# The head of an attention and feed-forward kernel on one core: k's maximum from transposes of k itself, parts of k^T v in zeroed tiles, w_out loaded two chunks later, loads issued in the order that the program tells

## The chip, the cores and the metric

The kernel runs on one core of a Trainium2 chip. A core has five engines, each with its own in-order queue of instructions: TensorE (PE; its weight loads are listed apart, as PEld), VectorE (DVE), ScalarE (ACT), GpSimd (POOL) and SyncE (SP), which here only issues DMAs. They meet by semaphores. The metric is the device time of one execution in microseconds (us), the median of several runs. Below, "batch" is the attention's batch (8 of them), and "chunk" is one of the 16 pieces of 128 that the feed-forward's inner width is cut into.

## What is computed

The reference, cut to what matters. Softmax runs over the head dimension for q and over the sequence for k; the result goes through a feed-forward layer with a squared ReLU. Everything is float32, except that w_in and w_out arrive as float64 (read as 64-bit words).

```
batch, n_heads, seq, head_dim = 8, 8, 576, 64        # x: 4608 tokens of 512; d_ff 2048
q_s = exp(q - max(q, axis=-1));  q_s = q_s / (sum(q_s, axis=-1) + 1e-9)
k_s = exp(k - max(k, axis=2));   k_s = k_s / (sum(k_s, axis=2) + 1e-9)
kv  = einsum('bhsd,bhse->bhde', k_s, v)
x   = einsum('bhsd,bhde->bhse', q_s, kv)             # then to (4608, 512)
h   = maximum(x @ w_in, 0.0)
out = h * h @ w_out
```

## The kernel before

**Tiles.** A batch of attention has four pairs of heads (p = 0..3). Of its 576 rows 512 are handled as 128 partitions x 4 rows (`c`), and the last 64 of all heads in "tail" tiles (`kt`, `qt`, `v_tail`). One feed-forward pass t handles 512 tokens: passes 0 to 7 take the main rows of batches 0 to 7, and pass 8 takes the 64-row tails of all batches.

**The feed-forward.** In pass t, for each chunk f, `first` (L467) makes h_f with 12 matmuls (four slices of x times three products of high and low parts: xh·wi_h, xl·wi_h, xh·wi_l). ACT takes the ReLU (r, L478) and the high part of its square (gh, L487); DVE makes the square (L479) and the low part (gl, L488). `second` (L491) adds chunk f-2 into four accumulators with 12 matmuls (gh·wo_h, gh·wo_l, gl·wo_h for each of four rows of tiles). The names in the profile are h, r, gh, gl, acc, with wi and wo for the weights.

**The weights.** Every chunk has one half from w_in ("i") and one from w_out ("o"), 512 KB of float64 each. `load_words` (L105) issues their DMAs on SP. `convert` (L159), called once for each half in turn, emits three steps: `scale_words` (two ACT operations, L125 and L126) for the next half, `join_words` (DVE L133 and L136, then DVE L141 for i or POOL L143 for o) for this one, and `split_words` (ACT cast L152, POOL subtraction L153) for the half before. A matmul of a chunk needs the L152 cast (high part) and the L153 subtraction (low part) of its half. The halves go i0, o0, i1, o1, ....

**The attention.** k's column maximum of a pair: DVE reduces over the four rows of a partition (`k_max`, L287), takes in the tail (L291), and then, for batches 0 and 1, `k_turn_max` (L316) transposes the 128x128 result on PE, reduces it to one column (kc, L322), makes a diagonal (dg, L324, DVE) and `k_shift_pe` multiplies it with ones so that the maximum stands in every partition (kmb, L332); DVE subtracts it (L301, L307). For later batches POOL does the partition maximum (L313). `k_exp` gives ek. `kv_product` (L385) makes k^T v in PSUM, scales it by one over the sum and zeroes the blocks off the diagonal with a mask (L406), and cuts it into kvh (ACT) and kvl (DVE). `x_product` makes x from them.

**What sets the order.** From pass 1 on the instructions stand as the code is written (`manual_schedule`, L636). Before that, for the head (all of batch 0's attention, called the boot, which runs in seven stages over the pairs) and pass 0 with batch 1's attention inside it, a scheduler sets the order of each engine at build time, so code that is moved shows only in the built order. In pass 0, `convert` is called twice for each chunk (L651, L661), and once each for the first four halves after the boot (L573). SP's queue is in order too: a DMA whose buffer is not free holds all that stands behind it. Batch 1's k, q and v have one buffer each, so pair 1's k is loaded when pair 0's ek has been made.

Of the kernel before, what the change touches and what calls it, by code (L numbers as in the profile page):

```python
# [22 lines left out]
def attention_ffn(  # L23
# [26 lines left out]
    P = 128  # L50
# [11 lines left out]
    LW = 2  # L62
    LD = 6
# [24 lines left out]
    mask = const.tile([P, P], F32, tag="mask", name="mask")  # L88
    nc.vector.memset(mask, 0.0)
    for j in range(2):  # L90
        nc.vector.memset(mask[j * D:(j + 1) * D, j * D:(j + 1) * D], 1.0)
# [13 lines left out]
    def load_words(f):  # L105
        pool = const if f < LATE else late
        for name, src in (
            ("i", w_in[:, f * P:(f + 1) * P].rearrange("(kc p) f -> p kc f", p=P)),
            ("o", w_out[f * P:(f + 1) * P, :]),
        ):  # L110
            raw = pool.tile([P, M], U64, tag=f"w{name}{f}", name=f"raw_{name}{f}")
            nc.sync.dma_start(
                out=raw if len(src.shape) == 2 else raw.rearrange("p (a b) -> p a b", b=P),
                in_=src,
            )
            raws.append((name, f, raw))
# [11 lines left out]
    def join_words(m):  # L128
        name, f, raw = raws[m]
        lo, hi = (raw.bitcast(I32).rearrange("p (n t) -> p n t", t=2)[:, :, i] for i in range(2))  # L130
        w = cvt.tile([P, M], I32, tag="w", name=f"w_{name}{f}")
        ps = bank(f"up_{name}{f}").bitcast(I32)
        nc.vector.tensor_scalar(  # L133
            out=ps, in0=hi, scalar1=3, scalar2=None, op0=ALU.logical_shift_left
        )
        nc.vector.scalar_tensor_tensor(  # L136
            out=ps if name == "i" else w, in0=hi, scalar=-(2**31), in1=ps,
            op0=ALU.bitwise_and, op1=ALU.bitwise_or,
        )
        if name == "i":  # L140
            nc.vector.tensor_tensor(out=w, in0=ps, in1=lo, op=ALU.add)  # L141
# [17 lines left out]
    def convert():  # L159
# [29 lines left out]
    def load_kq(b, p, which, queue=nc.sync):  # L189
        t = pair_tile(b, p, [P, 2, C, D], which)  # L190
        src = k if which == "k" else q
        queue.dma_start(
            out=t, in_=src[b, 2 * p:2 * p + 2, 0:M, :].rearrange("h (p c) d -> p h c d", c=C)
        )
# [88 lines left out]
    def k_max(b, p):  # L283
        kr = made["k", b, p]
        tl, th = tail_of(b, p)
        km = small([P, P], "km", f"km_{b}_{p}")
# [10 lines left out]
    def k_shift(b, p, kmx, eng):  # L297
# [17 lines left out]

    def k_turn_max(b, p):  # L316

        km = made.pop(("km", b, p))
        ps = bank(f"kmT_{b}_{p}")
        nc.tensor.transpose(out=ps[:, 0:P], in_=km, identity=ident)  # L320
        kc = small([P, 1], "kc", f"kc_{b}_{p}")
        nc.vector.tensor_reduce(out=kc, in_=ps[:, 0:P], op=ALU.max, axis=AX.X)  # L322
        dg = small([P, P], "dg", f"dg_{b}_{p}")
        nc.vector.tensor_scalar(  # L324
            out=dg, in0=ident, scalar1=kc, scalar2=None, op0=ALU.mult
        )
# [10 lines left out]
    def k_exp(b, p):  # L337
# [47 lines left out]
    def kv_product(b, p):  # L385
# [30 lines left out]
        nc.scalar.copy(out=kvh, in_=kv)  # L416
        nc.vector.tensor_tensor(out=kvl, in0=kv, in1=kvh, op=ALU.subtract)
# [100 lines left out]


# [11 lines left out]
    for f in range(LW):  # L531
        load_words(f)
    x = x_tiles(0)

    def boot_max(p):
        k_max(0, p)
        if p == 0:
            tail_exp(0)

    def boot_turn(p):  # L540
# [5 lines left out]
    def boot_exp(p):  # L546
# [7 lines left out]
        boot_max,  # L554
# [7 lines left out]
    for n in range(len(stages) + NP - 1):  # L562
# [3 lines left out]
        if n == len(stages) - 1:  # L566
# [4 lines left out]
            for f in range(LW, LD):  # L571
                load_words(f)
    for _ in range(2 * LW):  # L573
        convert()
# [59 lines left out]
    for t in range(B + 1):  # L634
        if t == 1:
            ctx.enter_context(tc.manual_schedule())  # L636
# [7 lines left out]
        for f in range(NF):  # L644
# [15 lines left out]
            if t == 0 and f + LW < NF:  # L660
# [47 lines left out]
```

## Time and profile before

| | us |
|---|---|
| median of 3 runs (lowest, highest) | 920.75 (920.45, 921.54) |
| the profiled execution | 920.5 |
| its span, first to last instruction | 918.7 |
| PE busy | 880.0 (96%) |
| DVE busy | 502.4 (55%) |
| ACT busy | 348.9 (38%) |
| POOL busy | 154.7 (17%) |
| mean granted TensorE clock | 0.992 |

The times below are microseconds from the start of the span. Busy shares over the whole span say little here, since the kernel has a head of some 155 us that is unlike the remaining 764 us: the stages have to be read one by one. A row of the timeline gives start, duration, engine, line, operation, what it writes and reads, and how many are merged. Instructions overlap in their pipelines, so the distance from one start to the next is shorter than the duration: two scalings of ACT that follow each other start 0.56 us apart, though each lasts 0.68 us.

### The profile page before, as it was taken

Reading aid. Unit: us, or ns where it says so; the run is one execution under the profiler, and the core shown is the slowest. Engines: PE = TensorE matmul, PEld = TensorE weight load, DVE = VectorE, ACT = ScalarE, POOL = GpSimd, SP = SyncE. Lnnn points to the kernel's source line nnn. Section 1 sums busy time; section 2 is a strip of 40 time slices with the busy share of each in tenths; the row PEclk is TensorE's granted clock in tenths of the full one; section 3 lists DMA queues with packets and bytes.
Section 4 is the critical chain, followed back from the end, with each engine's and each line's share of the span. In section 5 each row is a group of like instructions: output and inputs, shape, how many; then the busy total and the mean of one; then the engine's idle time right before and its main releaser. Section 6 shows DMA issues by size and latency. Waiting matters only on the chain.

```text
span 918.7 us, 11463 instructions
## 1 busy us (share of the span) xinstructions
PE 880.0 (96%) x4136; PEld 731.2 (80%) x4136; DVE 502.4 (55%) x982; ACT 348.9 (38%) x679; POOL 154.7 (17%) x238
## 2 busy tenths in 40 slices
PE   3598999999999999999999999999999999999997
PEld 2486778888888888888888888888888888888886
DVE  8978888654564447545745466454744442233222
ACT  3997445333343234333433343333423332232221
POOL 3366663101111111111111101111110100000000
PEclk9799999999999999999999999999999999999999
DMA  8990102111221122111311031112211020001001
GB/s 247 355 381 25 38 24 84 35 35 34 59 81 35 35 53 86 35 34 32 95 36 35 15 101 35 35 35 58 81 35 35 1 97 1 1 8 39 0 1 47
DMA packets 84937, 57.38 MB, mean 62 GB/s; under 512 B 53520, under 2 KB 78096, under 8 KB 84752
## 3 DMA queue, kind: packets, MB, share of 16 engines
q1 hardware_dynamic: 83168, 55.33, 19.6%
q10 hardware_dynamic: 1712, 1.31, 0.5%
q8 instruction: 33, 0.54, 0.2%
q14 instruction: 24, 0.20, 0.1%
HBM read 46.14 MB, written 10.49 MB: 62 GB/s over the span
## 4 chain that ended last, share of the span: by engine, by line
PE 81%; DVE 8%; ACT 7%; issue 2%; DMA 1%; POOL 1%; SPq 0%; DVEq 0%; ACTq 0%
PE h L473 38%; PE acc L495 37%; PE kv L391 2%; PE x L428 2%; PE qT L368 1%; DVE xl L464 1%; DVE gl L488 1%; ACT r L478 1%; DVE h L479 1%; ACT gh L487 1%; ACT raw_i L125 1%; ACT raw_i L126 1%; ACT raw_o L125 1%; DVE km L287 1%; ACT raw_o L126 1%
## 5 line engine op out<-in xcount | busy, mean ns | idle before, releaser
L473 PE MATMUL h<-xh,wi 128*128 128x512 f32 x1152 | 382.8, 395 | 5.3 <-ACT wi L152 5.0
L495 PE MATMUL acc<-wo,gh 128*128 128x512 f32 x1152 | 349.6, 390 | 3.5 <-ACT gh L487 3.4
L473 PEld LDWEIGHTS h<-xh,wi 128*128 128x128 f32 x1152 | 217.1, 189 | 53.1 <-ACT wi L152 5.9
L495 PEld LDWEIGHTS acc<-wo,gh 128*128 128x128 f32 x1152 | 215.1, 188 | 49.7 <-ACT gh L487 5.7
L473 PE MATMUL h<-xl,wi 128*128 128x512 f32 x576 | 225.7, 392 | 0.0
L495 PE MATMUL acc<-wo,gl 128*128 128x512 f32 x576 | 217.4, 389 | 0.0
L479 DVE SCALAR_TENSOR_TENSOR h<-h,r 128x512 f32<-128x512 f32 x144 | 100.6, 698 | 193.4 <-ACT r L478 192.7
L488 DVE TENSOR_TENSOR gl<-h,gh 128x512 fp32r<-128x512 f32 x144 | 99.5, 691 | 171.5 <-ACT gh L487 168.1
L478 ACT ACTIVATE r<-h 128x512 f32<-128x512 f32 x144 | 86.0, 597 | 219.2 <-PE h L473 219.1
L487 ACT ACTIVATE gh<-r 128x512 fp32r<-128x512 f32 x144 | 91.0, 632 | 196.8 <-PE acc L495 194.1
L495 PEld LDWEIGHTS acc<-wo,gl 128*128 128x128 f32 x576 | 108.0, 188 | 22.6
L473 PEld LDWEIGHTS h<-xl,wi 128*128 128x128 f32 x576 | 108.9, 189 | 20.8
L301 POOL TENSOR_TENSOR k<-k,kmx 128x512 f32<-128x512 f32 x24 | 31.0, 1291 | 172.6 <-issue 172.6
L313 POOL PARTITION_ALL_REDUCE kmx<-km x24 | 17.6, 734 | 226.8 <-DVE km L291 221.1
L391 PEld LDWEIGHTS kv<-v,ek 128*128 128x128 f32 x256 | 33.4, 195 | 4.5 <-ACT wi L152 2.4
L391 PE MATMUL kv<-v,ek 128*128 128x129 f32 x256 | 34.8, 279 | 2.2 <-ACT wi L152 2.0
L287 DVE TENSOR_REDUCE km<-k 128x128 f32<-128x512 f32 x32 | 33.9, 1059 | 2.7 <-DMA k<-in_k_dram 2.7
L342 ACT ACTIVATE ek<-k 128x512 f32<-128x512 f32 x32 | 20.1, 627 | 23.6 <-POOL k L301 16.7
L382 DVE TENSOR_TENSOR ql<-qT,qh 128x512 fp32r<-128x512 f32 x32 | 22.0, 688 | 6.8 <-ACT qh L381 6.8
L416 ACT CAST kvh<-kv 128x128 fp32r<-128x128 f32 x32 | 9.5, 298 | 39.3 <-DVE kv L406 39.1
L240 DVE TENSOR_REDUCE mx<-q 128x8 f32<-128x512 f32 x32 | 21.7, 679 | 2.7 <-DMA q<-in_q_dram 2.3
L464 DVE TENSOR_TENSOR xl<-x,xh 128x512 fp32r<-128x512 f32 x32 | 20.2, 687 | 5.4 <-ACT xh L463 5.3
(84 smaller groups left out, 675.2 us busy)
## 6 DMA issues: line engine op xcount, KB each, us to landing
k<-in_k_dram SPq DMA_DIRECT2D x32, 256.0 KB, 2.8
v<-in_v_dram SPq DMA_DIRECT2D x64, 128.0 KB, 3.1
raw_i<-in_moe_w_in_dram SPq DMA_DIRECT2D x16, 512.0 KB, 8.1
raw_o<-in_moe_w_out_dram SPq DMA_DIRECT2D x16, 512.0 KB, 7.9
out_dram<-o SPq DMA_DIRECT2D x32, 256.0 KB, 2.6
q<-in_q_dram SPq DMA_DIRECT2D x28, 256.0 KB, 2.9
q<-in_q_dram ACTq DMA_DIRECT2D x4, 256.0 KB, 4.7
kt<-in_k_dram SPq DMA_DIRECT2D x16, 64.0 KB, 2.7
```

What stands on the lines that cost most here:

```text
L240: nc.vector.tensor_reduce(out=mx, in_=t, op=ALU.max, axis=AX.X)
L287: nc.vector.tensor_reduce(out=km.rearrange("p (h d) -> p h d", h=2), in_=kr.rearrange("p h c d -> p h d c"), op=ALU.max, axis=AX.X,)
L301: eng.tensor_tensor(out=kr, in0=kr, in1=kmx.rearrange("p (h d) -> p h d", h=2).unsqueeze(2).broadcast_to([P, 2, C, D]), op=ALU.subtract,)
L382: nc.vector.tensor_tensor(out=ql[:, 0:M], in0=ps, in1=qh[:, 0:M], op=ALU.subtract)
L391: nc.tensor.matmul(out=ps[:, 0:W], lhsT=kr[:, c, :], rhs=vr[:, c, :], start=(c == 0), stop=False)
L464: nc.vector.tensor_tensor(out=lo, in0=src[:, p, :], in1=hi, op=ALU.subtract)
L473: nc.tensor.matmul(out=ps, lhsT=w[f][:, p * P:(p + 1) * P], rhs=m, start=(n == 0), stop=(n == 3 * NP - 1))
L478: nc.scalar.activation(out=r, in_=ps, func=AF.Relu)
L479: nc.vector.scalar_tensor_tensor(out=ps, in0=ps, scalar=0.0, in1=r, op0=ALU.max, op1=ALU.mult)
L487: nc.scalar.activation(out=gh, in_=r, func=AF.Square)
L488: nc.vector.tensor_tensor(out=gl, in0=ps, in1=gh, op=ALU.subtract)
L495: nc.tensor.matmul(out=acc[c], lhsT=a[:, cs], rhs=w[f], start=(f == 0 and n == 0), stop=(f == NF - 1 and n == 2),)
```

## The change

Four things are changed, all in the head and in what it shares with later batches.

1. **k's maximum.** For batches 0 and 1, `k_max` goes. k is loaded as (row, head, d) instead of (head, row, d), so that each of the four rows of a pair is a 128x128 block; PE transposes all four into one PSUM bank (kT), and one DVE reduction over 512 gives the column kc. The tail's maximum comes from two transposes for each batch (`k_tail_max`, ktT and ktm), and is taken in by an operation on 128x1. The diagonal dg is made by ACT. The subtraction and division of q's tail move from DVE to POOL for these batches.
2. **k^T v.** The mask goes. Two pairs of tiles, kvh and kvl, are zeroed once by POOL; ACT writes the scaled 64x64 diagonal blocks into kvh, and DVE the rest into kvl, straight from PSUM. This holds for all eight batches.
3. **Halves.** The list `halves` goes i0, i1, i2, o0, i3, o1, ...: w_out's half of a chunk stands behind w_in's half two chunks later. Four halves are loaded early, eight more in the boot, then two in each chunk; the first four conversions are called in the last stages of the boot, and i0 and i1 are joined with POOL.
4. **DMA issues.** SP follows the written order from the start of the program.

The core of the diff (before.py to after.py):

```diff
+    EARLY = 4
+    AHEAD = 12
...
+    halves = [("i", f) for f in range(LA)]
+    for f in range(NF):
+        halves += [("i", f + LA)] * (f + LA < NF) + [("o", f)]
+    def load_words(n):
+        for name, f in halves[len(raws):len(raws) + n]:
...
+        on_vector = name == "i" and f >= LA
-        if name == "i":
+        if on_vector:
             nc.vector.tensor_tensor(out=w, in0=ps, in1=lo, op=ALU.add)
         else:
             nc.gpsimd.tensor_tensor(out=w, in0=w, in1=lo, op=ALU.add)
...
+        turned = which == "k" and b < 2
+        t = pair_tile(b, p, [P, C, 2, D] if turned else [P, 2, C, D], which)
...
+        rows_max(qt, G, f"t{b}", nc.vector if b > 1 else nc.gpsimd)
...
+    def k_tail_max(b):
+        ps = bank(f"ktT_{b}")
+        for i in range(2):
+            nc.tensor.transpose(
+                out=ps[:, i * P:(i + 1) * P],
+                in_=made["kt", b][:, 2 * i:2 * i + 2, :].rearrange("p h d -> p (h d)"),
+                identity=ident,
+            )
+        ktm = small([P, NP], "ktm", f"ktm_{b}")
+        nc.vector.tensor_reduce(
+            out=ktm, in_=ps[:, 0:2 * P].rearrange("p (n t) -> p n t", t=TL), op=ALU.max, axis=AX.X
+        )
     def k_turn_max(b, p):
-        km = made.pop(("km", b, p))
-        nc.tensor.transpose(out=ps[:, 0:P], in_=km, identity=ident)
+        kr = made["k", b, p].rearrange("p c h d -> p c (h d)")
+        for c in range(C):
+            nc.tensor.transpose(
+                out=ps[:, c * P:(c + 1) * P], in_=kr[:, c, :], identity=ident
+            )
-        nc.vector.tensor_reduce(out=kc, in_=ps[:, 0:P], op=ALU.max, axis=AX.X)
+        nc.vector.tensor_reduce(out=kc, in_=ps, op=ALU.max, axis=AX.X)
+        nc.vector.tensor_tensor(
+            out=kc, in0=kc, in1=made["ktm", b][:, at:at + 1], op=ALU.max
+        )
-        nc.vector.tensor_scalar(
-            out=dg, in0=ident, scalar1=kc, scalar2=None, op0=ALU.mult
-        )
+        nc.scalar.activation(out=dg, in_=ident, func=AF.Copy, scale=kc)
...
+        kvh, kvl = kv_parts[(b * NP + p) % 2]
         for j in range(2):
+            at = slice(j * D, (j + 1) * D)
+            one = ps[at, j * (D + 1):j * (D + 1) + D]
+            nc.scalar.activation(out=kvh[at, at], in_=one, func=AF.Copy, scale=ks[at])
             nc.vector.scalar_tensor_tensor(
...
+                out=kvl[at, at], in0=one, scalar=ks[at], in1=kvh[at, at],
+                op0=ALU.mult, op1=ALU.subtract,
             )
...
+    order = ExitStack()
+    order.enter_context(tc.manual_schedule(engines={mybir.EngineType.SP}))
...
             load_v(1, 0)
-            for f in range(LW, LD):
-                load_words(f)
-    for _ in range(2 * LW):
-        convert()
+            load_words(AHEAD - EARLY)
+        if n >= len(stages) + NP - 1 - EARLY:
+            convert()
...
-            if t == 0 and f + LD < NF:
-                load_words(f + LD)
-            if t == 0 and f + LW <= NF:
+            if t == 0:
+                load_words(2)
                 convert()
```

Where the scheduler puts things, at the two places that matter most below. The first is ACT's queue just ahead of the cast of chunk 0's w_in half (wi0); a name like raw_i3 is the float64 words of w_in's half for chunk 3, xh_0_3 the high part of x of pair 3 of batch 0, kvh1 the second zeroed tile. Before:

```order
L126 ACTIVATE raw_i3_382<-raw_i3_382 128x512
L447 COPY xt_0_329<-x_0_2_1_440 128x64
L125 ACTIVATE raw_o3_384<-raw_o3_384 128x512
L126 ACTIVATE raw_o3_384<-raw_o3_384 128x512
L435 CAST xh_0_3_158<-x_0_3_0_458 128x288
L435 CAST xh_0_3_158<-x_0_3_1_464 128x224
L125 ACTIVATE raw_i4_386<-raw_i4_386 128x512
L126 ACTIVATE raw_i4_386<-raw_i4_386 128x512
L125 ACTIVATE raw_o4_388<-raw_o4_388 128x512
L126 ACTIVATE raw_o4_388<-raw_o4_388 128x512
L125 ACTIVATE raw_i5_390<-raw_i5_390 128x512
L152 CAST wi0_488<-w_i0_476 128x512
```

and in the changed program:

```order
L457 CAST xh_0_0_160<-x_0_0_0_328 128x288
L457 CAST xh_0_0_160<-x_0_0_1_334 128x224
L408 CAST qh_0_2_429<-qT_0_2_424 128x512
L133 ACTIVATE raw_i1_154<-raw_i1_154 128x512
L408 CAST qh_0_1_347<-qT_0_1_342 128x512
L134 ACTIVATE raw_i1_154<-raw_i1_154 128x512
L435 ACTIVATE kvh0_93<-kv_0_2_353,ks_0_2_359 64x64
L133 ACTIVATE raw_i2_156<-raw_i2_156 128x512
L134 ACTIVATE raw_i2_156<-raw_i2_156 128x512
L469 COPY xt_0_340<-x_0_0_1_334 128x64
L161 CAST wi0_455<-w_i0_406 128x512
```

The cast of wi0 stood behind the scaling of ten halves and a half (i0 to o4, and the first step of i5), and now stands behind three (i0, i1, i2); it also stands ahead of all casts of x but pair 0's.

The second place is SP's queue from the twelfth weight half on; x_tail is the store of the tails of x, v_tail the load of batch 1's tail of v, k_1_1 and v_1_1 the loads of pair 1 of batch 1. Before, all weight loads but one stood ahead of x_tail and of pair 1:

```order
L112 DMA raw_o5_392<-in_moe_w_out_dram 128x512
L223 DMA v_tail_98<-in_v_dram 64x2x64 x4
L112 DMA raw_i6_554<-in_moe_w_in_dram 128x4x128
L112 DMA raw_o6_556<-in_moe_w_out_dram 128x512
L112 DMA raw_i7_616<-in_moe_w_in_dram 128x4x128
```

Now:

```order
L123 DMA raw_o4_400<-in_moe_w_out_dram 128x512
L471 DMA x_tail_103<-xt_0_340 512x1x64
L232 DMA v_tail_104<-in_v_dram 64x2x64 x4
L121 DMA raw_i7_561<-in_moe_w_in_dram 128x4x128
L123 DMA raw_o5_563<-in_moe_w_out_dram 128x512
L121 DMA raw_i8_627<-in_moe_w_in_dram 128x4x128
L123 DMA raw_o6_629<-in_moe_w_out_dram 128x512
L203 DMA k_1_1_648<-in_k_dram 128x8x64
L203 DMA q_1_1_650<-in_q_dram 128x2x256
L121 DMA raw_i9_678<-in_moe_w_in_dram 128x4x128
L123 DMA raw_o7_680<-in_moe_w_out_dram 128x512
L210 DMA v_1_1_739<-in_v_dram 128x4x64 x2
```

Twenty weight halves now stand behind x_tail, which waits for the whole boot; sixteen of them stand behind k_1_1, which waits for ACT to make pair 0's ek of batch 1, and fourteen behind v_1_1, which waits for PE's k^T v of that pair.

The third place is ACT's queue around the ReLU of chunk 5 (r_0_5), in the changed program; x_1 is the copy of x for the next pass, wo3 and wi6 the casts of weights.

```order
L133 ACTIVATE raw_i10_769<-raw_i10_769 128x512
L134 ACTIVATE raw_i10_769<-raw_i10_769 128x512
L500 ACTIVATE r_0_5_917<-h_0_5_904 128x512
L133 ACTIVATE raw_o8_771<-raw_o8_771 128x512
L134 ACTIVATE raw_o8_771<-raw_o8_771 128x512
L464 COPY x_1_536<-x_1_0_0_799 128x288
L161 CAST wo3_780<-w_o3_745 128x512
```

At chunk 5 before, ACT had all 32 halves scaled; now the scaling of i10 and o8 stands ahead of the cast of wo3, which PE needs as soon as h_5 is done.

More of the change, by code (lines that the diff above doesn't have):

```diff
@@ L87, in attention_ffn @@
     nc.vector.memset(ones, 1.0)
[L88 to L91, printed above, removed]
+    zeros = const.tile([P, P], F32, tag="zeros", name="zeros")
+    nc.gpsimd.memset(zeros, 0.0)
+    kv_parts = []
+    for i in range(2):
+        kv_parts.append([const.tile([P, P], F32R, tag=f"kv{c}{i}", name=f"kv{c}{i}") for c in "hl"])
+        for part in kv_parts[-1]:
+            nc.gpsimd.tensor_copy(out=part, in_=zeros)
     dram = ctx.enter_context(tc.tile_pool(name="dram", bufs=1, space=bass.MemoryType.DRAM))
@@ L103, in attention_ffn @@
     raws = []
[L105 to L114, printed above, removed]
-            )
+    halves = [("i", f) for f in range(LA)]
[3 more added lines that the diff above has]
+        for name, f in halves[len(raws):len(raws) + n]:
+            raw = (const if f < LATE else late).tile(
+                [P, M], U64, tag=f"w{name}{f}", name=f"raw_{name}{f}"
+            )
+            if name == "i":
+                src = w_in[:, f * P:(f + 1) * P].rearrange("(kc p) f -> p kc f", p=P)
+                nc.sync.dma_start(out=raw.rearrange("p (a b) -> p a b", b=P), in_=src)
+            else:
+                nc.sync.dma_start(out=raw, in_=w_out[f * P:(f + 1) * P, :])
             raws.append((name, f, raw))
@@ L189, in load_kq @@
     def load_kq(b, p, which, queue=nc.sync):
[L190 to L193, printed above, removed]
-        )
+        turned = which == "k" and b < 2
+        t = pair_tile(b, p, [P, C, 2, D] if turned else [P, 2, C, D], which)
+        src = (k if which == "k" else q)[b, 2 * p:2 * p + 2, 0:M, :]
+        to = "p c h d" if turned else "p h c d"
+        queue.dma_start(out=t, in_=src.rearrange(f"h (p c) d -> {to}", c=C))
         made[which, b, p] = t
@@ L285, in k_max @@
         tl, th = tail_of(b, p)
-        km = small([P, P], "km", f"km_{b}_{p}")
+        km = small([P, P], "km", f"km_{b}_{p}", 1)
         nc.vector.tensor_reduce(
@@ L530, in attention_ffn, with boot_turn @@
         load_v(0, p)
-    for f in range(LW):
-        load_words(f)
+    load_words(EARLY)
     x = x_tiles(0)
-    def boot_max(p):
-        k_max(0, p)
+    def boot_turn(p):
         if p == 0:
+            k_tail_max(0)
             tail_exp(0)
-    def boot_turn(p):
         k_turn_max(0, p)
@@ L635, in attention_ffn @@
         if t == 1:
+            order.close()
             ctx.enter_context(tc.manual_schedule())
@@ L659, in attention_ffn @@
                 step_after(b, f, x_next)
-            if t == 0 and f + LW < NF:
+            if t == 0:
                 convert()
```

52 lines of the change are left out of this document (19 added, 33 removed).

## The prediction

> **What bounds the kernel now.** I read first the busy times by stage, then PE's timeline at the borders of the stages, then who PE waits for between them. The first view: columns are length, then busy time and count of PE, PEld, DVE, ACT and POOL, the granted clock, the DMA share and GB/s.
>
> ```profile
> 0.00:41.90 41.90, 16.92 (x95) 13.65 (x95) 37.51 (x107) 26.68 (x60) 13.56 (x30) 0.90 0.93 291
> 41.90:50.60 8.70, 8.70 (x28) 6.40 (x28) 8.21 (x15) 8.30 (x16) 8.70 (x8) 0.68 1.06 399
> 50.60:68.50 17.90, 17.85 (x87) 14.73 (x86) 12.98 (x24) 17.90 (x36) 9.36 (x11) 1.00 1.07 385
> 68.50:155.00 86.50, 79.88 (x376) 64.37 (x375) 74.17 (x141) 46.11 (x90) 52.12 (x50) 1.00 0.12 33
> 155.00:918.70 763.70, 756.68 (x3556) 632.01 (x3554) 369.55 (x699) 249.87 (x481) 71.00 (x142) 1.00 0.14 42
> ```
>
> From 155 on PE is busy 756.7 of 763.7 us at full clock, and nothing in the change takes a matmul out of that stage: it stays as it is. All that can move lies ahead of 155. There PE is idle 25 us before 41.9, and 6.6 us between 68.5 and 155.
>
> PE's timeline at the borders: the first feed-forward matmul, the end of the first two chunks (h_0, h_1), and the point where pass 0 has been added up and pass 1 runs on alone.
>
> ```profile
> 41.89 0.80 PE L473 MATMUL h<-xh,wi 128*128 128x512 f32 x1 [4.30 <-ACT wi L152]
> 50.34 0.38 PE L332 MATMUL kmb<-dg,ones 128*128 128x128 f32 x2
> 155.02 0.39 PE L473 MATMUL h<-xh,wi 128*128 128x512 f32 x1
> ```
>
> The first matmul waits for ACT's cast of wi0, and ACT's timeline shows why that is late:
>
> ```profile
> 20.13 0.68 ACT L125 ACTIVATE raw_i<-raw_i 128x512 f32<-128x512 f32 x1
> 20.69 0.68 ACT L126 ACTIVATE raw_i<-raw_i 128x512 int32<-128x512 uint32 x1
> ...
> 40.52 0.24 ACT L447 COPY xt<-x 128x64 f32<-128x64 f32 x1
> 40.62 0.72 ACT L125 ACTIVATE raw_i<-raw_i 128x512 f32<-128x512 f32 x1
> 41.18 0.65 ACT L152 CAST wi<-w_i 128x512 fp32r<-128x512 f32 x1
> ```
>
> The words of i0 were scaled at 20.13, and cast 21 us later; ACT scaled other halves meanwhile. DVE, 37.5 of 41.9 us busy, was late as well: it made w_i0 only at 40.19 (next fence). So the head is bound by the order of work on ACT and DVE, not by loads.
>
> **The change, term 1: the first two chunks come earlier.** The built order has wi0's cast behind 3 scaled halves instead of 10.5. Two scaling steps start 0.56 us apart (20.13 and 20.69), so a half is 1.12 us and 7.5 halves are 8.4 us of ACT. The casts of x of pairs 1 to 3 and their neighbours, some 3.3 us, also stand behind it now. On ACT alone the cast could stand at 41.2 - 8.4 - 3.3 = 29.5. DVE must keep up:
>
> ```profile
> 40.19 0.67 DVE L141 CUSTOM_DVE_ANT_0 w_i<-raw_i,up_i 128x1024 uint16<-128x1024 uint16 x1
> L287 DVE TENSOR_REDUCE km<-k 128x128 f32<-128x512 f32 x32 | 33.9, 1059 | 2.7 <-DMA k<-in_k_dram 2.7
> L291 DVE TENSOR_TENSOR km<-km,kt 64x128 f32<-64x128 f32 x32 | 9.1, 285 | 1.5 <-DMA kt<-in_k_dram 0.6
> L324 DVE TENSOR_SCALAR dg<-ident,kc 128x128 f32<-128x128 f32 x8 | 4.9, 608 | 0.2
> L322 DVE TENSOR_REDUCE kc<-kmT 128x1 f32<-128x128 f32 x8 | 2.3, 283 | 1.0 <-PE kmT L320 0.9
> L240 DVE TENSOR_REDUCE mx<-q 128x8 f32<-128x512 f32 x32 | 21.7, 679 | 2.7 <-DMA q<-in_q_dram 2.3
> L241 DVE TENSOR_TENSOR qt<-qt,mx_t 128x256 f32<-128x256 f32 x8 | 3.4, 422 | 0.2
> L153 POOL TENSOR_TENSOR wi<-w_i,wi 128x512 fp32r<-128x512 f32 x16 | 20.7, 1295 | 2.7 <-ACT wi L152 2.7
> ```
>
> Ahead of w_i0 DVE loses five L287 (1.06 each), five L291 (0.28), four L324 (0.61) and four operations on q's tail (0.42, as L241): 10.8 us. It gains four kc over 512 elements instead of 128; no row shows that reduction from PSUM, so I take L240's 0.68 for the same 128x512 (bounds: 0.28, as now, and L287's 1.06), and a few short ones: 4 x 0.4 + 0.9 = 2.5 us. Some 7 us of batch 1's reductions and other halves' joins move behind w_i0. That is 15 us less: w_i0 at about 26, POOL's addition after it (1.3 us, as its 128x512 subtraction) at 27.5. ACT's 29.5 is the later of the two. The dg on ACT (four) and the split kvh (two 64x64 for one 128x128) are not in the trace; between the 0.24 of L447 and the 0.65 of a 128x512 cast I take 0.25 each, 2 us, most of it in ACT's idle time before 20. **First matmul at 30** (28 to 33).
>
> PE then runs h_0 and h_1 over pairs 0 to 2 and waits for pair 3, whose casts stand behind i3 and o1 on ACT: three more halves (3.4 us), the wi1 cast and the 3.3 us from above put xh_3 at 36 to 37, DVE's low part 0.7 behind, and the last matmuls at **39** (37 to 43), against 50.34 + 0.2 = 50.6. **Term 1: -11.6.**
>
> **Loads.** A k load now lands in pieces of 256 bytes instead of 1 KB. The first window below holds mostly 1 KB pieces, the second v alone, in 256-byte pieces; the last three columns are clock, DMA share, GB/s.
>
> ```profile
> 8.00:11.00 3.00, 0.41 (x2) 0.18 (x1) 3.00 (x7) 1.76 (x4) 0.55 (x1) 1.00 1.07 319
> 11.50:15.00 3.50, 0.39 (x1) 0.18 (x1) 3.44 (x8) 1.26 (x2) 1.04 (x1) 1.00 0.59 133
> ```
>
> For the same busy engines v moves 133/0.59 = 225 GB/s against 319/1.07 = 298. Four k loads of 0.26 MB then take 4.7 instead of 3.5 us: 1.2 us, hidden behind DVE, which by the new order takes q's two maxima (0.68 and about 0.4) ahead of the first kc; without that cover it costs the 1.2 us. The Trainium skill, "DMA: Bandwidth & Descriptors", section Specifications, says that line rate needs pieces of at least 512 B; the trace agrees in direction (225 against 298), and by it alone the change would start about 1 us later, which is inside the range of term 1.
>
> **Term 2: more on PE.** Batch 0's extra transposes fall into PE's idle time. Batch 1's, inside pass 0, are on the path: 12 more for the four pairs and 2 for the tail.
>
> ```profile
> 95.40 0.44 PE qT L368 x4
> ```
>
> Four transposes took 0.44 in the chain of waits; twelve are 1.3 us (the tail's two run while PE waits for pair 3). **Term 2: +1.3.**
>
> **Term 3: the waits of pass 0.** Between 50.5 and 155 PE waits for these, longest first:
>
> ```profile
> PE acc L495 <- ACT gh L487: 3.4, 3, 1.8
> PE kv L391 <- ACT wi L152: 2.0, 1, 2.0
> PE h L473 <- ACT wi L152: 0.7, 1, 0.7
> PE kmb L332 <- DVE dg L324: 0.3, 1, 0.3
> PE kv L391 <- issue: 0.2, 1, 0.2
> ```
>
> That is 6.6 us. I walked the new order by hand with the durations above and four more from the chain of waits (start, length, engine, tile, line):
>
> ```profile
> 63.05 0.53 ACT gh L487
> 65.80 0.47 ACT r L478
> 67.84 0.52 ACT wo L152
> 101.36 0.85 PE x L428 x6
> ```
>
> Five waits stand out. (a) After h_1 ACT still has r_0, r_1, the scaling of i5, gh_0 and wo0's cast, 2 x 0.47 + 1.12 + 0.53 + 0.52 = 3.1 us, and PE only 0.5 us of transposes: 2.5 us. (b) wo1's low part is POOL's third task in a row of 1.3 us: 1 to 2. (c) Around chunk 5 ACT has i10 and o8 ahead of wo3's cast: PE has x_product's 0.85 us and waits 2 to 3. (d) The same at chunk 9 with wo7: 1.5 to 2.5. (e) At the end of pass 0 the last x_product now stands right before the matmuls of pass 1 that read it, and its copy, cast and low part take 1.7; before, 2.7 us of matmuls lay in between. Sum 8.7 to 11.7; I take 9.5, and the old 6.6 go. **Term 3: +2.9** (-4 if PE finds ACT ahead everywhere but in (a), +6 at the upper ends with late loads).
>
> The late loads: the told order holds 20 halves behind x_tail, and 16 of them behind pair 1's k.
>
> ```profile
> 56.70 1.97 SPq L449 DMA_DIRECT2D x_tail<-xt  x1
> DMA to landing us min/median/max: 4.3/8.1/9.5
> ```
>
> x_tail's issue took 1.97 us and a w_in half landed 4.3 us after its issue at best. With x_tail released at about 39, i7 lands at 48, when ACT reaches it at 46 to 47. Pair 1's k is released by ek at 56, and i9 lands at 62; ACT, behind chunk 4's ReLU, would reach it at 59. ACT so waits 1.5 and 3 us, with everything in its queue behind; (c) includes that. The second hold (pair 2's, i13) is alike, and (d) includes it.
>
> **Term 4: later passes.** The split kvh and kvl hand over four times instead of twice, a chunk before x_product reads them: nothing (bounds -0.3 and +1.5). DVE and ACT have half their time free there.
>
> **Sum.** -11.6 + 1.3 + 2.9 = -7.4 against this execution's own 920.5 (span 918.7 and 1.8 around it; the median of the runs is 920.75): **913**.
>
> **Rivals.** (1) *PE finds its operands ready.* DVE is 10 us lighter, so the joins may run far ahead; then only (a) and (e) remain: waits of 4.2, -12.7: 908. For it: DVE was the one 74 of 86.5 us busy in that stage. Against it: ACT's new row keeps scaling to chunk 10. (2) *The change does little:* DVE or a late k keeps w_i0 until 36. Then term 1 is -6 and the sum -2: 918.5. For it: DVE was nearly never idle before 40. (3) *Slower:* the told order starves ACT. If each of the four held groups (behind x_tail, and pairs 1, 2 and 3's k and v) costs PE 5 us instead of 1 to 3, waits are 20 or more; it turns slower when they pass 9.5 + 7.4 = 17. Released a chunk late (6.8 us) twice: 913 + 13.6 = 926.5. For it: SP's queue is in order and ACT's too, so one late half stops ReLUs behind it; against it: between 68.5 and 155 the DMA share is 0.12, so a released load goes at once. (4) *PE at half rate.* The clock by the granted-clock column:
>
> ```profile
> 30.00:32.00 2.00, 0.80 (x4) 0.59 (x4) 2.00 (x7) 1.65 (x7) 1.08 (x1) 1.00 1.07 379
> 34.00:36.00 2.00, 1.33 (x4) 0.98 (x4) 2.00 (x5) 2.00 (x6) 0.00 (x0) 0.50 1.05 407
> 46.00:48.00 2.00, 2.00 (x7) 1.59 (x6) 1.97 (x5) 1.88 (x4) 2.00 (x3) 0.64 1.04 391
> 48.00:50.00 2.00, 2.00 (x11) 1.65 (x10) 1.68 (x3) 1.72 (x4) 2.00 (x2) 1.00 1.05 404
> ```
>
> After a thin stretch from 29 the clock fell to 0.50, and came back 5 us after matmuls ran densely; 13 matmuls then cost 0.2 us more each. The new head has thin stretches too, and (a) is one: half rate over the first three chunks would add 13 x 0.2 and as much again, less what the waits hide, about 3.5 us: 916.5. The Trainium skill, "TensorE: Matmul & The Clock Gate", section "What's actually happening", puts the fall at an idle window of about 3.4 us; (a)'s 2.5 would be just short of it, and the trace's fall after five thin microseconds fits.
>
> **How the numbers follow.** Forecast 913: 0.60; (1) 908: 0.14; (2) 918.5: 0.10; (3) 926.5: 0.07; (4) 916.5: 0.09. The forecast's own range, from the bounds of terms 1 and 3, is 908 to 918. The range 906.5 to 919.5 takes in (1), (2) and (4) with their spread, and leaves out (3) and the edges. A measurement can tell 0.2%, 1.8 us: faster than 918.7 are the forecast, (1), (4) and half of (2), 0.88, less 0.03 for the forecast's upper tail: 0.85; within 0.2% that tail and the other half of (2), 0.08; slower (3), 0.07.
>
> **What would show it.** First h matmul at 28 to 33 and the end of h_1 at 37 to 43; (a) of 2 to 3 us on PE before the first acc, for wo0's cast; waits for wo3 and wo7 after chunks 5 and 9; SP idle before k_1_1 for ek; pass 1's lone stretch from about 147.5 instead of 155.02; the rest of the span 763.7 as now. It would be wrong if h_0 starts after 35, if pass 0's waits exceed 14 us, or if the stage after it changes length by over 2 us.

## The result: slower, 928.03 us, and the profile after

The changed kernel takes **928.03 us** (median of 5, 927.62 to 928.50) against 921.54 for the kernel before (median of 5, 920.45 to 924.20): ratio **1.0067, 95% interval 1.0050 to 1.0085**. The profiled execution has a span of 925.8, against 918.7. The forecast was 913, with a range up to 919.5.

The busy times by stage of the changed kernel, with the columns as in the prediction:

```profile
0.00:32.10 32.10, 19.12 (x102) 16.39 (x102) 24.46 (x69) 19.59 (x44) 16.96 (x38) 1.00 0.92 236
32.10:41.50 9.40, 9.06 (x36) 7.11 (x36) 8.86 (x23) 9.32 (x23) 5.95 (x6) 0.82 0.96 354
41.50:68.50 27.00, 23.23 (x103) 18.45 (x102) 18.28 (x35) 21.42 (x43) 13.00 (x14) 0.94 0.64 198
68.50:155.00 86.50, 79.75 (x369) 65.13 (x369) 74.28 (x129) 54.56 (x107) 53.13 (x50) 0.96 0.33 104
155.00:925.80 770.80, 762.53 (x3555) 633.45 (x3555) 367.03 (x675) 260.10 (x506) 71.82 (x143) 1.00 0.15 42
```

The clock column is below 1.00 in the three stages from 32.10 to 155, where the kernel before had it below 1.00 only ahead of 50.6, and the last stage is 7.1 us longer. PE's timeline at the borders and at its waits (the wait and who ended it stand in brackets):

```profile
32.15 0.50 PE L495 MATMUL h<-xh,wi 128*128 128x512 f32 x1 [2.43 <-DVE xl L458]
40.93 0.60 PE L344 MATMUL kT<-ident,k 128*128 128x128 f32 x4
43.93 1.90 PE L517 MATMUL acc<-wo,gh 128*128 128x512 f32 x4 [2.40 <-ACT wo L161]
70.25 0.37 PE L450 MATMUL x<-qh,kvh 128*128 128x288 f32 x1 [3.02 <-DVE kvl L436]
72.21 0.58 PE L450 MATMUL x<-qh,kvh 128*128 128x288 f32 x1 [1.32 <-ACT x L464]
101.34 0.37 PE L450 MATMUL x<-qh,kvh 128*128 128x288 f32 x1 [1.19 <-DVE w_o L145]
103.27 0.38 PE L450 MATMUL x<-qh,kvh 128*128 128x288 f32 x1 [1.29 <-DVE w_i L150]
156.04 0.50 PE L495 MATMUL h<-xh,wi 128*128 128x512 f32 x1 [1.90 <-ACT xh L485]
```

The head came as forecast: h_1 ends at 40.9 and not at 50.3, 9.4 us earlier. To see where that went I take a mark that both kernels have, the two transposes of q's tail in chunk 2 of pass 1 (the first fence is the kernel before, the second the changed one; the second line of each is the group of all such transposes, whose last is in pass 6):

```profile
163.87 0.38 PE L268 MATMUL qTt<-ident,qt 128*128 128x128 f32 x2
L268 PE MATMUL qTt<-ident,qt x16: 270/271/476, 17.8 to 653.1; 128*128 128x128 f32 x16
```

```profile
167.15 0.39 PE L277 MATMUL qTt<-ident,qt 128*128 128x128 f32 x2
L277 PE MATMUL qTt<-ident,qt x16: 270/273/474, 11.6 to 658.7; 128*128 128x128 f32 x16
```

So the changed kernel is 9.4 ahead at the end of h_1, 3.3 behind at the start of pass 1, 5.6 behind in pass 6 and 7.1 behind at the end. **Pass 0 gives back 12.7 us, and the passes behind it, which I had at nothing, lose another 3.8.**

**Pass 0.** PE's groups between 41 and 165, with the idle time ahead of each (the last figures of a row):

```profile
L495 PE MATMUL h<-xh,wi 128*128 128x512 f32 x137 | 47.7, 412 | 2.0 <-ACT xh L485 1.9
L517 PE MATMUL acc<-wo,gh 128*128 128x512 f32 x130 | 45.5, 419 | 2.7 <-ACT wo L161 2.7
L495 PE MATMUL h<-xl,wi 128*128 128x512 f32 x68 | 27.9, 410 | 0.2 <-DVE xl L486 0.2
L450 PE MATMUL x<-qh,kvh 128*128 128x288 f32 x8 | 2.9, 359 | 6.8 <-DVE kvl L436 3.0 <-ACT x L464 1.3 <-DVE w_i L150 1.3
```

That is 11.7 us, 5.1 more than the 6.6 before, and the largest part stands ahead of x_product, which waited for nothing in the kernel before. Then the clock, in the three stretches behind the longest waits:

```profile
44.00:48.00 4.00, 3.90 (x10) 2.60 (x11) 4.00 (x7) 4.00 (x9) 2.80 (x3) 0.57 0.65 174
70.00:80.00 10.00, 8.42 (x28) 6.83 (x29) 7.10 (x13) 8.59 (x18) 5.37 (x6) 0.66 0.39 150
156.00:162.00 6.00, 5.74 (x17) 4.39 (x18) 3.83 (x8) 1.86 (x4) 1.04 (x1) 0.72 0.55 197
```

(1 - 0.57) x 4 + (1 - 0.66) x 10 + (1 - 0.72) x 6 = 6.8 us, of which some 0.3 is idle time counted already. In the kernel before the same column was 1.00 from 50.6 on. With the 1.3 us of more transposes (the forecast's figure) and 0.5 for slower matmuls (next) that makes 5.1 + 6.5 + 1.3 + 0.5 = 13.4, near the 12.7 that the marks show. The clock's share in it is worked out and not tested: no run changes the clock alone.

**The later passes.** The chain of waits in pass 7, in which there is no attention, of the changed kernel and then of the kernel before (start, length, matmuls). The first row is h of chunk 12; the accumulation of a chunk comes two chunks later, so that the last row is the accumulation of chunks 13 to 15:

```profile
805.52 2.80 PE h L495 x12
808.32 2.75 PE acc L517 x12
...
822.18 2.80 PE h L495 x12
824.98 8.40 PE acc L517 x36
```

```profile
799.56 2.72 PE h L473 x12
802.28 2.72 PE acc L495 x12
...
815.88 2.72 PE h L473 x12
818.60 8.16 PE acc L495 x36
```

From the start of the first row to the end of the last it is 27.86 us against 27.20. The matmuls that use the weights of chunks 12 to 15 are issued 3% more slowly (233 ns for 227), in every pass, with no wait between them and the clock at 1.00; the chunks ahead run as before, but for the accumulation rows between such rows (2.75), whose ends border on them. From the mark in pass 1 to that in pass 6 it is 0.46 us a pass; 8 passes of 0.46 to 0.66 make 3.7 to 5.3, which covers the 3.8 that the later passes lost.

### The profile page after: what moved, and what is told of

Read it like the earlier page. It is cut to its first block, busy times and chain, and to the rows that moved or that the text cites. A ratio compares the mean times of both kernels' runs of the same rounds, so it can differ in the third digit from the quotient of the medians.

```text
span 925.8 us, 11627 instructions
## 1 busy us (share of the span) xinstructions
PE 893.7 (97%) x4164; PEld 740.5 (80%) x4164; DVE 492.9 (53%) x927; ACT 365.0 (39%) x719; POOL 160.9 (17%) x249
## 4 chain that ended last, share of the span: by engine, by line
PE 87%; ACT 6%; DMA 3%; DVE 2%; issue 1%; SPq 0%; POOL 0%; DVEq 0%; ACTq 0%
PE acc L517 40%; PE h L495 40%; PE x L450 2%; PE kv L418 2%; PE qT L395 1%; DMA k<-in_k_dram 1%; ACT raw_i L133 1%; ACT raw_i L134 1%; DMA raw_o<-in_moe_w_out_dram 1%; DMA raw_i<-in_moe_w_in_dram 1%; ACT raw_o L133 1%; ACT raw_o L134 1%; ACT r L500 1%; ACT gh L509 1%; PE kv L421 0%
## 5 line engine op out<-in xcount | busy, mean ns | idle before, releaser
L517 PE MATMUL acc<-wo,gh 128*128 128x512 f32 x1152 | 361.4, 393 | 2.7 <-ACT wo L161 2.7
L517 PE MATMUL acc<-wo,gl 128*128 128x512 f32 x576 | 225.8, 392 | 0.0
L435 ACT ACTIVATE kvh<-kv,ks 64x64 fp32r<-64x64 f32 x64 | 19.8, 310 | 39.5 <-PE qT L395 20.1
L436 DVE SCALAR_TENSOR_TENSOR kvl<-kv,ks,kvh 64x64 fp32r<-64x64 f32 x64 | 18.1, 283 | 20.9 <-ACT kvh L435 20.5
L450 PE MATMUL x<-qh,kvh 128*128 128x288 f32 x64 | 19.7, 311 | 7.4 <-DVE kvl L436 3.0
L296 DVE TENSOR_REDUCE km<-k 128x128 f32<-128x512 f32 x24 | 25.6, 1065 | 0.5 <-DMA k<-in_k_dram 0.5
```

The source lines that it names most:

```text
L296: nc.vector.tensor_reduce(out=km.rearrange("p (h d) -> p h d", h=2), in_=kr.rearrange("p h c d -> p h d c"), op=ALU.max, axis=AX.X,)
L450: nc.tensor.matmul(out=ps[:, 0:SH], lhsT=a, rhs=c[:, cs], start=(j == 0), stop=(j == 2))
L517: nc.tensor.matmul(out=acc[c], lhsT=a[:, cs], rhs=w[f], start=(f == 0 and n == 0), stop=(f == NF - 1 and n == 2),)
```

## The experiments

The ratios are each to the kernel before in the same comparison.

| kernel | us | ratio (95%) |
|---|---|---|
| changed | 928.03 | 1.0067 (1.0050 to 1.0085) |
| pad | 927.25 | 1.0077 (1.0064 to 1.0089) |
| before_off | 925.22 | 1.0053 (1.0041 to 1.0066) |
| pad256 | 922.99 | 1.0022 (1.0011 to 1.0033) |
| kold | 929.54 | 1.0082 (1.0065 to 1.0099) |
| kvold | 919.99 | 0.9987 (0.9975 to 0.9998) |
| halold | 917.63 | 0.9963 (0.9951 to 0.9976) |
| free_sp | 933.58 | 1.0145 (1.0132 to 1.0159) |
| ahead16 | 928.63 | 1.0093 (1.0080 to 1.0107) |
| a16d | 921.65 | 0.9995 (0.9982 to 1.0008) |
| kv16 | 916.43 | 0.9949 (0.9936 to 0.9963) |
| **kv16d** | **915.41** | **0.9937 (0.9925 to 0.9950)** |
| hal16d | 916.39 | 0.9951 (0.9935 to 0.9966) |

### Where the late weights lie: pad, before_off, pad256

Chunks 12 to 15 are those whose weights lie in the pool `late`, allocated behind the small pool `tiny`. The change puts a new small tile, ktm, into `tiny`: two slots of 32 bytes. That moves `late`, and with it the tiles of the boot, which lie in the same place until `late` is opened. The addresses of wi12 in the built programs, in bytes of a partition:

```
before      190720 = 745 x 256          pad         189312 = 739 x 256 + 128
changed     189248 = 739 x 256 + 64     before_off  190784 = 745 x 256 + 64
                                        pad256      189440 = 740 x 256
```

The edit is one number, here that of pad (48 in before_off too, 80 in pad256); the instructions and their order stay the same:

```
-    tiny.tile([P, 32], F32, tag="pad2", name="pad2")
+    tiny.tile([P, 48], F32, tag="pad2", name="pad2")
```

> The changed kernel with the small pool made 64 bytes longer, so that the late pool (the parts of wi12 to wo15) starts on a multiple of 128 bytes again, as it did before; the order of all instructions is the same. Theory A (addresses): the 24 matmuls of each of chunks 12 to 15 are issued 231 ns apart in the changed kernel and 227 in the kernel before; 96 x 9 passes x 4.5 ns = 3.9 us, so 924.1 (928.03 - 3.9), and the last 20 us back to 227 ns. Rival (the later passes are longer through the split kv parts' extra handovers and the wait for ks): no change, 928, chunks 12 to 15 stay at 231.

> The kernel before with the small pool made 64 bytes longer, so that its late pool starts 64 bytes beside a multiple of 128; the order of all instructions is the same. Theory A: chunks 12 to 15 go from 227 to 231 ns a matmul, +3.9 us, 925.4 against 921.5. Rival (the addresses are without effect; the edits of k and kv cost it): 921.5.

pad did not do what theory A said: 927.25, and its last accumulation in pass 7 still takes 8.40. before_off did: 4.9 us slower by the ratio. That row of before_off, from its chain of waits:

```profile
823.66 8.40 PE acc L495 x36
```

So the address matters, but a multiple of 128 isn't enough. The constants' weights lay on multiples of 256 in both kernels, hence:

> As pad, but the small pool is 192 bytes longer than in the changed kernel, so that wi12 to wo15 start on a multiple of 256 bytes, as all weights of the kernel before did (with 128 bytes beside such a multiple, in pad, their matmuls stayed at 231 ns). Same order of instructions as the changed kernel. Theory A, mended (the weights want a multiple of 256 bytes): chunks 12 to 15 at 227 ns in all passes, 3.9 us less, 924.1, and from pass 1's first qTt to the end as long as before, 655 instead of 658.6. Rival (something else than the address, e.g. the split kv parts): 928.

pad256 came as forecast, with the same row back at the old length:

```profile
820.40 8.16 PE acc L517 x36
```

From the mark in pass 1 to the end of the span it takes 755.4 us; the changed kernel took 758.65 (925.8 - 167.15), the kernel before 754.8 (918.7 - 163.87). The rest of the gain, some 1 to 2 us, lies ahead of the mark (165.11 against 167.15), where the same waits came out a little otherwise; before_off lost 2.6 us there, with a half-clock stretch at 118 to 122 that the kernel before did not have. Why is open.

### The parts one by one: kold, kvold, halold

kold and kvold undo one part each in pad256; halold undoes one more in kvold.

```
kold     -  transposes of the four blocks of k, ktT, dg on ACT, k loaded as "p c h d"
         +  k_max on DVE, one transpose a pair, dg on DVE, k loaded as "p h c d"
kvold    -  kvh[at, at] on ACT and kvl[at, at] on DVE for each of two blocks, tiles zeroed once
         +  kv with the mask on DVE, kvh one cast on ACT, kvl one difference on DVE
halold   -  i0, i1, i2, o0, i3, o1, ...
         +  i0, o0, i1, o1, ...
```

> pad256 with k's maximum as before the change (on DVE over k as loaded in long pieces, one transpose a pair, diag on DVE); the told order, the parts of kv and the order of the halves stay. If the new maximum brings the early head (my term 1), the first h comes at 36 to 38 instead of 32 and the time is 4 to 6 us above pad256; rival (the order of the halves alone brings it, and the 12 transposes and ACT's diag cost): the first h stays near 32 and the time is 1 to 3 us below pad256.

kold: the first feed-forward matmul moves from 31.73 in pad256 to 42.58, later than forecast, and the time rises by 0.60%, 5.5 us. The new maximum makes the early head. It is worth half of what the head gains: of the 10.9 us only 2.5 are left at the mark in pass 1 (165.11 in pad256, 167.60 in kold), and 4.9 more come behind the mark in these two executions, which differ by 7.4, where kold waits for batch 2's ek (see ahead16 below). k_max is a boot stage of its own again in kold, as before the change.

```profile
42.58 0.63 PE L488 MATMUL h<-xh,wi 128*128 128x512 f32 x1
```

> pad256 with the parts of k^T v as before the change (masked product on DVE, one cast on ACT, one difference on DVE); the rest stays. If the handovers ACT-DVE-ACT-DVE of the split parts hold x_product in pass 0 (PE waits 3.0 for kvl at 67 to 70 in the changed kernel), that wait falls to below 1 and the time is 2 to 4 us below pad256. Rival (that wait is ACT's wait for i9, told order): within 1.5 us of pad256, the wait stays.

kvold: 0.35%, 3.2 us faster than pad256, and faster than the kernel before. The group of x_product in pass 0 waits 0.6 us in place of 6.8 in the changed kernel, though ACT's wait for raw_i is no shorter (4.0 us, 3.8 in pad256), so the rival is out:

```profile
L452 PE MATMUL x<-qh,kvh 128*128 128x288 f32 x8 | 2.6, 320 | 0.6 <-ACT kvh L440 0.6
```

The timelines of ACT and DVE in the changed kernel show how the split parts wait (two fences, ACT and then DVE):

```profile
66.55 0.30 ACT L435 ACTIVATE kvh<-kv,ks 64x64 fp32r<-64x64 f32 x1
66.76 0.65 ACT L133 ACTIVATE raw_o<-raw_o 128x512 f32<-128x512 f32 x1
...
68.49 0.31 ACT L435 ACTIVATE kvh<-kv,ks 64x64 fp32r<-64x64 f32 x1
```

```profile
67.41 0.27 DVE L436 SCALAR_TENSOR_TENSOR kvl<-kv,ks,kvh 64x64 fp32r<-64x64 f32 x1
...
69.81 0.29 DVE L436 SCALAR_TENSOR_TENSOR kvl<-kv,ks,kvh 64x64 fp32r<-64x64 f32 x1
```

Four operations of 0.3 us take from 66.55 to 70.10, since other work (scaling of weights and gh on ACT, joins and gl on DVE) stands between the two on each engine, and PE's x_product at 70.25 needs the last. In the profiled executions kvold reaches the mark 3.9 us before pad256 (161.19) and gives 2.6 of them back behind it.

> kvold with the halves in the order before the change (i0, o0, i1, o1, ...) in place of the new one, in which halves of w_out stand two chunks later. If the new order brings the early head, wi1 is now a half later and h_1 ends 2 us or more after kvold's 41.1, and the time is 2 to 4 us above kvold, 922 to 924. Rival (the new order only moves the wait from wi1 to wo0, at the first acc): h_1 ends later, the wait before the first acc falls from 3.4 to about 1, and the time is within 1.5 us of kvold.

halold: 0.24%, 2.2 us faster than kvold, with intervals that just overlap. Neither time came: the first theory had it slower, the rival within 1.5 us. The first acc of kvold, and then that of halold:

```profile
45.09 3.41 PE L519 MATMUL acc<-wo,gh 128*128 128x512 f32 x8 [3.37 <-ACT gh L511]
```

```profile
45.63 2.42 PE L519 MATMUL acc<-wo,gh 128*128 128x512 f32 x8
```

The last matmul of h_1 starts at 40.89 in kvold and at 45.21 in halold, and yet the accumulation starts at 45.09 and 45.63: what the new order gains at h_1, PE waits for the square of h. In these executions halold reaches the mark 0.5 us later than kvold (161.73), and its gain lies behind it (755.7 us to the end against 758.0). So the 2.2 us are not shown to be a cost of the order in pass 0.

### The told order: ahead16, free_sp, a16d, kv16, kv16d, hal16d

In the changed kernel i9 stands behind pair 1's k on SP. SP's timeline and then ACT's:

```profile
56.85 0.63 SPq L203 DMA_DIRECT2D k<-in_k_dram  x1
...
58.27 0.46 SPq L121 DMA_DIRECT2D raw_i<-in_moe_w_in_dram  x1
```

```profile
64.44 0.67 ACT L133 ACTIVATE raw_i<-raw_i 128x512 f32<-128x512 f32 x1 [3.60 <-DMA raw_i<-in_moe_w_in_dram]
```

The edits: `AHEAD = 16` for 12 (ahead16); no `manual_schedule` for SP (free_sp); both on pad.

> As pad, with 16 instead of 12 halves loaded ahead of the first chunk, so that i9 and o7 stand ahead of pair 1's k on SP, and i13 ahead of pair 2's. Theory B (the told order holds weights behind k, ACT waits, and what stands behind it on ACT holds PE): ACT's waits of 3.6 and 1.5 us for raw_i go, PE's waits of 3.0, 1.3, 1.2 and 1.3 us at 67 to 72 and 100 to 103 go, and the half clock at 72 to 78 (3 us): about 9 us less than pad, 915. Rival C (ACT has too much to do there in any case: scaling, casts, dg, kvh): the waits stay and move from the load to the casts; within 2 us of pad.

> As pad, without the told order on SP: the scheduler puts all weight halves ahead of pair 1's k, q and v. Theory B: ACT no longer waits for raw_i, gain as with 16 ahead, 915, unless k of pair 1 now comes late (its wait then stands at the transposes of pair 1's k or at ek). Rival C: within 2 us of pad.

free_sp is slower, 933.58 against 927.25 in pad: the told order as such is no mistake. All weights go ahead of pair 1's k, ACT no longer waits for raw_i, and PE's waits in pass 0 are about as long as in pad (13 and 12 us, of which 5.8 and 6.0 at x_product); its mark comes at 167.57, 1.5 us before pad's, and what it loses in its profile lies behind that, where PE waits for batch 2's ek:

```profile
170.83 2.03 PE L418 MATMUL kv<-v,ek 128*128 128x129 f32 x8 [2.88 <-ACT ek L371]
```

The two executions profiled differ by 2.7 us, the medians by 6.3; the rest is not accounted for. ahead16's time looks like no gain, 928.63, but its profile shows one that is given back. ACT's wait for raw_i falls from 5.3 in pad to 1.6, pad's half-clock stretches at 74 to 78 and 104 to 110 go, and the mark in pass 1 comes at 162.63 against 169.04 in pad, 6.4 us earlier. Right behind it PE waits:

```profile
165.00 1.16 PE L418 MATMUL kv<-v,ek 128*128 128x129 f32 x8 [1.99 <-ACT ek L371]
...
167.57 0.69 PE L395 MATMUL qT<-ident,qn 128*128 128x128 f32 x2 [1.03 <-DVE qtl L285]
```

and goes on at half clock. POOL's timeline of the same execution says why ek is late:

```profile
147.69 1.29 POOL L162 TENSOR_TENSOR wo<-w_o,wo 128x512 fp32r<-128x512 f32 x1 [1.76 <-ACT wo L161]
154.62 0.72 POOL L321 PARTITION_ALL_REDUCE kmx<-km  x1 [5.64 <-DMA x_tail<-xt]
163.04 1.25 POOL L314 TENSOR_TENSOR k<-k,kmx 128x512 f32<-128x512 f32 x1 [7.70 <-issue]
```

Batch 2's maximum over the partitions starts 5.6 us after POOL's last conversion, and the subtraction of it 8 us later. km was ready at 149.45, 5.2 us before the maximum starts; in a16d, the next kernel, it is ready only 2.0 us before, and the maximum again starts 5.6 us after POOL's last instruction. So the 5.6 run from that instruction, not from the data. a16d takes that last conversion away from POOL (and puts the late weights on 256 bytes):

```
-        nc.gpsimd.tensor_tensor(out=lo, in0=w, in1=hi, op=ALU.subtract)
+        (nc.vector if m == 2 * NF - 1 else nc.gpsimd).tensor_tensor(out=lo, in0=w, in1=hi, op=ALU.subtract)
```

> pad256 with 16 halves loaded ahead, and wo15's low part made by DVE instead of POOL, whose last conversion it was; the rest of the order is that of ahead16 but for two matmuls. In ahead16 pass 0 ended 6.4 us earlier than in pad, and PE then waited 2.0 and 1.0 for ek and qtl of batch 2's first pair, at half clock after. Theory D (the early end of pass 0 is lost to POOL: its maximum over the partitions starts 5.7 us after POOL's last conversion in every run, and k's shift, ek and the first kv follow it): POOL is free at 145.9 instead of 149.0, the first kv of pass 1 no longer waits, so 3 us of waits and some 2 to 3 us of half clock less than ahead16, and 3.9 less by the addresses: 928.6 - 3.9 - 5.5 = 919. Rival (the load of k's tail, or ACT and DVE, hold it): the waits stay, 924.5.

a16d: 921.65, between the two, so by its time alone it settles nothing. By its profile theory D holds: the first kv of pass 1 follows the mark without a wait.

```profile
163.84 0.38 PE L277 MATMUL qTt<-ident,qt 128*128 128x128 f32 x2
164.06 1.06 PE L418 MATMUL kv<-v,ek 128*128 128x129 f32 x8
```

Against pad256, from which it differs by the 16 halves and this edit alone, it gains 0.27%, 2.5 us.

The other profiles fit the same chain. Where the shift of batch 2's first k on POOL starts 1.8 us or more before the mark and the late weights lie on multiples of 256 bytes (before, pad256, halold, a16d and the three kernels below), the stretch from the mark to the end takes 754.7 to 755.7 us. In kvold the shift starts 1.1 us before the mark and the stretch takes 758.0; in kold it starts 0.1 behind it, and 760.3. In free_sp (1.3 behind) and ahead16 (0.4 behind), whose late weights are off, it is 762.9 and 764.2, against 758.8 in pad. Only a16d edits this chain; for the others it is an agreement and not a test.

> kvold (the parts of k^T v as before the change, late weights on a multiple of 256 bytes) with 16 instead of 12 halves loaded ahead. Theory B (the told order holds i9 and i13 behind k; the splits of kv are a second, separate cost): ACT's waits for raw_i fall to under 2 us and the time is 1 to 3 us below kvold's 920.0, 917 to 919. Rival (once the split parts are gone, ACT is late for other reasons and the held loads cost nothing; or POOL's maximum at the start of pass 1 gives it back, as in ahead16): 919.5 to 922.

> kv16 with wo15's low part on DVE instead of POOL. Theory D: the first kv of pass 1 does not wait for ek, and the time is up to 3 us below kv16 where kv16 waits there, and the same where it does not; 916 to 919. Rival: no difference to kv16.

kv16: 0.38%, 3.5 us below kvold, and a little below the range forecast for it; ACT's wait for raw_i falls from 4.0 to 1.4 us. In the profiled executions 1.6 us of the gain lie ahead of the mark (159.61) and 3.0 behind it, where kv16's shift on POOL comes in time. kv16d has the lowest median of all, **915.41, 0.63% below the kernel before**; the step from kv16, 0.12%, lies inside the intervals, and kv16 had no wait at ek to lose. Two stages of its pass 0, against the third and fourth of the changed kernel:

```profile
41.50:68.50 27.00, 23.62 (x110) 19.48 (x109) 20.89 (x40) 27.00 (x54) 14.93 (x15) 0.94 0.96 315
68.50:155.00 86.50, 83.01 (x398) 68.09 (x397) 75.02 (x139) 50.86 (x100) 50.72 (x50) 1.00 0.26 80
```

From 68.5 to 155 PE is busy 83.0 us at full clock, in place of 79.75 at 0.96.

> kv16d with the halves in the order before the change, as in halold: of the change there are left k's maximum on TensorE and the told order, with 16 halves ahead. If the costs add (the new order of the halves cost 2.4 us between kvold and halold), 915.4 - 2.4 = 913. Rival (with 16 ahead the order of the halves no longer matters, since both hold enough weights ready): 915 to 916.5.

hal16d: 916.39, as the rival said. With 16 halves ahead and wo15 moved, the order of the halves is worth nothing that shows.

## Why the prediction was wrong, by its steps

In us of the span the sum had -11.6 for the head, +1.3 for the transposes, +2.9 for the waits, nothing for the clock and nothing for the later passes: -7.4. The traces show -9.4, +1.3 (not isolated), +5.1, +6.5 for the clock, +0.5 for slower matmuls in pass 0 and +3.8 behind it, nearly all of that from the late weights: +7.8, where +7.1 was measured. So the steps that failed are the two terms put at nothing, the clock behind the waits of pass 0 and the speed of the matmuls on the late weights; after them come the waits and the head, each 2.2 us off. With the addresses, the split parts and the held loads put right, kv16d takes 915.4, 2.4 us above the forecast: these three hold most of the 15 us that were missed, the clock that fell behind their waits included.

- **Bound, and what moves: wrong in one half.** "It stays as it is" was said of the stage after pass 0. No instruction in it got a new wait of weight, but chunks 12 to 15 of every pass became slower by their address (pad256, before_off). No term had it; term 4, with its range from -0.3 to +1.5, was for the split parts alone, and with the addresses put right the stretch behind the mark is 0.6 us longer than before (755.4 and 754.8), inside that range. The addresses cost 3.2 us behind the mark, by pad256 against the changed kernel and by before_off against the one before. The cause was a tile of 16 bytes in a small pool (two slots of 32), in a line of the diff that I had read as arithmetic only.
- **Term 1, -11.6: right, a little high.** The first matmul came at 32.15 (28 to 33), h_1 ended at 40.9 (37 to 43): -9.4. The cast of wi0 stood at 29.46, as forecast (29.5), but then PE waited for the low part of x on DVE (xl, the bracket at 32.15), a wait that the term did not have. kold shows that the new maximum makes the early head, and that of kold's 10.9 us only 2.5 reached pass 1, where the sum carried term 1 over in full.
- **Loads, and term 2, +1.3:** no run isolated them. The account of pass 0 comes out 0.7 us above the marks with 1.3 in it, so it asks for no more.
- **Term 3, +2.9: too small.** (a) 2.40 against 2.5 and (e) 2.1 against 1.7 came where said. (b) did not come. (c) and (d) came at chunks 5 and 9, 4.3 and 2.8 against 2 to 3 and 1.5 to 2.5, but nearly all at x_product, not at the accumulations. In all 11.7 us against 9.5. What failed is the line "The split kvh and kvl hand over four times ...: nothing": it was priced for the later passes, where it holds (between the marks in pass 1 and pass 6 a16d, with the split parts, and kv16d, without them, both take 489.2 us), and I never priced it for pass 0, where ACT and DVE are full of conversion. kvold puts it at 3.2 us, the clock that fell behind these waits included.
- **Late loads: right for pair 1, not for the others.** ACT waited 3.6 for i9 (3 forecast). For i13, said to be alike, it waited 1.5, and the 1.5 forecast for i7 did not come. kv16 against kvold puts what the held loads cost at 3.5 us, without the split parts.
- **Rival (4), half clock: right as a mechanism, put in the wrong place.** I priced 3.5 us for the first three chunks. It came behind three waits of pass 0, 6.5 us by the clock column, only one of them in those chunks. The sum had nothing for it, and the rival a chance of 0.09. How much of the 6.5 the next wait would have taken anyway, no run separates.
- **Rival (3), slower, 926.5 with 0.07:** its time was near by luck: its condition (waits beyond 17 us) was not met; 11.7 of waits were enough, together with the clock and the addresses.
- **The signs of being wrong:** h_0 did not start after 35, nor did the waits pass 14 us; the third sign came, a change of over 2 us in the stage behind pass 0.

## What to carry to other kernels

A new tile in a pool can move what is allocated behind it, as ktm moved the late weights here: after such an edit, compare the spacing of the main loop's matmuls chunk by chunk before looking for waits. Where an edit splits an operation between two in-order engines, price every handover in the stage in which those engines are fullest, by what stands in their queues between the halves, and not by the operations' own length. A gain at the start lasts only as far as the next chain that doesn't depend on it (here POOL's maximum at the start of pass 1), so follow the new, earlier finish to the first thing that is still late.

## What the runs showed of the hardware

- 128x512 matmuls that read wi or wo at 64 or 128 bytes beside a multiple of 256 are issued at 233 ns against 227 (8.40 and 8.16 us for 36), at the same granted clock. It shows in busy time, not in waits. In the rows of h only the stationary operand (wi) is off, in those of acc only the moving one (wo), and both are slow by as much. Why, and at which other offsets, no run tells.
- The clock's fall isn't decided by the length of a wait alone. kv16 waited 3.40 us ahead of its first acc and kept 1.00; kv16d waited 3.38 at the same place and fell, and pad256 fell after 2.04 at the end of pass 0. One row of kv16, one of kv16d and two of pad256, by windows of 2 us:

```profile
42.00:44.00 2.00, 0.00 (x0) 0.00 (x0) 2.00 (x4) 2.00 (x5) 2.00 (x3) 1.00 1.05 395
```

```profile
46.00:48.00 2.00, 2.00 (x6) 1.61 (x5) 1.97 (x5) 2.00 (x5) 0.14 (x1) 0.50 1.15 298
```

```profile
152.00:154.00 2.00, 0.00 (x0) 0.00 (x0) 1.20 (x4) 1.20 (x4) 0.00 (x0) 1.00 0.18 39
156.00:158.00 2.00, 2.00 (x6) 1.61 (x5) 1.45 (x3) 1.56 (x3) 0.00 (x0) 0.50 0.96 371
```

  In the clock records of all fourteen traces a stretch at half clock lasts 3.41 us, or two or four times that, but for the one that the end of the program cuts off.

  The Trainium skill, "TensorE: Matmul & The Clock Gate", section "What's actually happening", has a free-running window of about 3.4 us that must be idle. That the phase counts agrees with these rows; that a whole window must be idle doesn't, with 2.04 us of idle time in pad256 (and 0.23 a little later).
- POOL's maximum over the partitions starts 5.5 to 6.0 us after the instruction ahead of it on POOL in batch 2, the first that POOL does, in all fourteen kernels. The Trainium skill, "GPSIMD Engine Reference", section "2.1 Instruction dispatch", gives about 6 us for loading code at the first call of a kernel; the length agrees. What it doesn't lead one to expect is the gap behind: from the start of this maximum to POOL's next instruction it is 8.4 us (154.62 to 163.04 in ahead16), and 7.6 to 8.3 in the next three of this kernel and of the changed one. The profile does not show what fills either gap.
